# Deferred sums, roots on GpSimd, fewer token riders and one more slot in a fused attention and gated-FFN kernel

## The chip, the cores and the metric

The kernel runs on one core of one Trainium2 chip. The metric is the device time of one execution in microseconds (us); of several runs the median is given. Each engine of the core works through its own queue in order: TensorE (PE) multiplies matrices, VectorE (DVE), ScalarE (ACT) and GpSimd (POOL) work elementwise, and SyncE (SP) issues nearly all transfers.

## The reference

2048 tokens of 512 features are normalised. One branch is a causal attention over a window of 256 keys, with 32 heads of 16 features; the other is a gated FFN with 1792 hidden features. The output is the input plus the product of the attention's projection and the silu of the FFN.

```python
xn = _layernorm(x)
s = _A_ref(xn, A_wqkv, A_wo)                  # softmax over keys i-255..i, then @ wo
g = _silu(_B_ref(xn, B_w1, B_w3, B_w2))       # (silu(xn @ w1) * (xn @ w3)) @ w2
return x + s * g
```

## The kernel before

**Numbers.** Every fp32 operand is held as a sum of two scaled fp16 numbers, high and low, and each dense product is three fp16 products (high-high, high-low, low-high). The split is done by ACT (high part) and by DVE or POOL (low part, a subtraction in two halves of 256 columns, L304).

**Tiles.** There are four token tiles t of 512 tokens, four groups g of 8 heads, and two halves p of a group: 32 *units* (t, g, p). A unit has two attention passes. Pass 1 (L575) computes scores with queries on the partitions and takes their maxima on DVE (L607). Pass 2 (L648) computes the scores again with keys on the partitions, adds masks on DVE (L676), takes exponentials on ACT (L679), and multiplies by the values into a PSUM tile of two banks called po (L697), of which there is one buffer. Pass 1 of a unit runs two units ahead of its pass 2. Pass 1 writes its scores to the tile s, which has two buffers, or, for the kinds marked "X" in the plan (L1065 and on), to po while that is free.

**A unit's end.** `finish` (L703) has ACT copy the first bank of po to os (L707), DVE add the second (L710), and SP store four blocks to the tile on (L716) and the denominators to DRAM (L717). With the second half of a group, `normalise` (L727) loads the denominators back; 8 steps later DVE inverts them (L734, L735) and they are broadcast by eight transfers to rb (L741); 24 steps later POOL has multiplied, and ACT and POOL split the result for the output projection (L747).

**Order.** PE's order is the order in which the program is written; the other engines' instructions are put in order by a scheduler when the program is built, by readiness and priority (`urgent`, L134, raises it). The program interleaves each unit's batches of scores with *dense pieces* of the FFN, projections and outputs (`spread`, L1097). Each batch and each piece is a *step*; `later(n, f)` (L140) emits f after n steps. The FFN's hidden features come in 14 blocks f: `gate_up` (L862), then `down` in four groups of blocks (L911), whose results are evicted at L932 and L935. In the first token tile the weights are loaded, measured (squares on ACT, L232 and L820) and split, and the split ones are stored to DRAM (dW); the later token tiles load them from there, `load` (L761) two blocks ahead: two tiles of w1 and w3 (L765) and one of w2 (L766).

**Slots.** Weights, products and sums share a pool of 39 slots of 2 KB a partition (`take`, L109), which are given back at a step of the program and taken oldest first. A transfer into a slot waits on SP until the slot's last readers have ended.

**Later tokens.** `prepare_beside` (L481) brings in token tiles 1 to 3 beside the units: loads, statistics (L404, L405), `rstd` (L407, a reciprocal square root by an integer guess, L409 to L414, and two steps of refinement on DVE, L416 to L424), centring (L427), and the transposition by small matmuls (L465) which *ride* on the unused columns of a pass-1 score tile, with two DVE instructions each (L474, L475). Which score tile takes a rider is decided in `pass1` (L596 to L603): one that finds `alone[0]` set; it is cleared by a rider unless the group's number t*4+g is at most 4.

Of the kernel before, what the change touches and what calls it, by code (L numbers as in the profile page):

```python
# [10 lines left out]
F32 = mybir.dt.float32  # L11
# [38 lines left out]
TWO_ONES = struct.unpack("f", struct.pack("ee", ONE, ONE))[0]  # L50
VW = DH + 1
VB = 10
SLOTS = 39
ORDERED = {ENGINE.PE}
GROUPS = ((0, 4), (4, 8), (8, 11), (11, 14))

# [23 lines left out]
def tile_block(ctx: ExitStack, tc: tile.TileContext, x, wqkv, wo, w1, w3, w2, out):  # L80
# [53 lines left out]
    def urgent():  # L134


        return tc.high_priority(offset=200) if started else nullcontext()
    made_so_far = [0]

    def later(n, f):  # L140
        made_so_far[0] += 1
        queue.append((now[0] + n, made_so_far[0], f))
# [249 lines left out]
    def prepare(t):  # L392

        mv = lnpool.tile([P, 4, 2], F32, name="mv")
        rs = lnpool.tile([P, 4], F32, name="rs")
        xts = {}

        def load(b):
            xts[b] = take(F32)
            (nc.scalar if t == 0 and b % 2 else nc.sync).dma_start(xts[b], x[t * TW + b * P:t * TW + (b + 1) * P, :])  # L400

        def stats(b):
            st = lnpool.tile([P, nc.vector.BN_STATS_DIM], F32, name="st")
            nc.vector.bn_stats(st, xts[b])  # L404
            nc.vector.bn_aggr(mv[:, b, :], st)  # L405

        def rstd(b0, b1):  # L407
            ve = lnpool.tile([P, b1 - b0], F32, name="ve")
            nc.vector.tensor_scalar(ve, mv[:, b0:b1, 1], 1e-5, None, op0=ALU.add)  # L409


            r0 = lnpool.tile([P, b1 - b0], F32, name="r0")
            nc.vector.tensor_scalar(r0.bitcast(I32), ve.bitcast(I32), 1, None, op0=ALU.logical_shift_right)
            nc.vector.tensor_scalar(r0.bitcast(I32), r0.bitcast(I32), -1.0, float(0x5F3759DF), op0=ALU.mult, op1=ALU.add)  # L414
            sq = lnpool.tile([P, b1 - b0], F32, name="sq")
            nc.vector.tensor_mul(sq, r0, r0)  # L416
            nc.vector.tensor_mul(sq, sq, ve)

            nc.vector.scalar_tensor_tensor(sq, sq, -10 / 3, sq, op0=ALU.add, op1=ALU.mult)
            nc.vector.scalar_tensor_tensor(r0, sq, 5.0, r0, op0=ALU.add, op1=ALU.mult)  # L420
            with nullcontext() if t else tc.issue_after(lasts["cast"].ins):
                nc.vector.tensor_mul(sq, r0, r0)
            nc.vector.scalar_tensor_tensor(sq, sq, -0.5 * (3 / 8)**3 * XS, ve, op0=ALU.mult, op1=ALU.mult)
            nc.vector.scalar_tensor_tensor(rs[:, b0:b1], sq, 1.5 * (3 / 8) * XS, r0, op0=ALU.add, op1=ALU.mult)  # L424

        def centre(b):
            lasts["centre"] = nc.vector.tensor_scalar(xts[b], xts[b], mv[:, b, 0:1], rs[:, b:b + 1],  # L427
                                                      op0=ALU.subtract, op1=ALU.mult)

        def turn(b):  # L430
            if t not in X:
                X[t] = xpool.tile([P, NC, TW], F16, name="XH"), xpool.tile([P, NC, TW], F16, name="XL")
            xh, xl = X[t]
            c = slice(b * P, (b + 1) * P)

            if b < 2:
                pt = bank([P, NC, P])
            elif b == 2:
                pt = pso.tile([P, 2, TW], F32, name="po")[:, 0, :].rearrange("p (k q) -> p k q", q=P)
            else:  # L440
                pt = scores_bank()[:, 0, :].rearrange("p (k q) -> p k q", q=P)
            for k in range(NC):
                nc.tensor.transpose(pt[:, k, :], xts[b][:, k * P:(k + 1) * P], identf)
            give(xts.pop(b))
            with urgent():
                lasts["xh"] = nc.scalar.copy(xh[:, :, c], pt)

            def rest():
                turned[t] = turned.get(t, 0) + 1
                with urgent():  # L450
                    lasts["x"] = nc.vector.tensor_sub(xl[:, :, c], pt, xh[:, :, c])
            later(1, rest)

        def turn_beside(b, n, s):


            if t not in X:
                X[t] = xpool.tile([P, NC, TW], F16, name="XH"), xpool.tile([P, NC, TW], F16, name="XL")
            xh, xl = X[t]
            for k in range(n, n + 2):  # L460
                for h in range(2):
                    for c in range(2):
                        f = k * P + 64 * c
                        rows = slice(64 * h, 64 * h + 64)
                        nc.tensor.matmul(s[64 * c:64 * c + 64, h, WIN + 64 * (k - n):WIN + 64 * (k - n + 1)],  # L465
                                         xts[b][rows, f:f + 64], identf[rows, rows], start=True, stop=True)
            if n:
                give(xts.pop(b))

            def rest():  # L470
                pt = s[:, :, WIN:WIN + P].rearrange("p h (k q) -> p k h q", k=2)
                hi, lo = (a[:, n:n + 2, b * P:(b + 1) * P].rearrange("p k (h q) -> p k h q", h=2) for a in (xh, xl))
                with urgent():
                    nc.vector.tensor_copy(hi, pt)  # L474
                    nc.vector.tensor_sub(lo, pt, hi)  # L475
                if n:
                    turned[t] = turned.get(t, 0) + 1
            return rest
        return load, stats, rstd, centre, turn if t == 0 else turn_beside
# [95 lines left out]
    def pass1(t, g, p):  # L575
# [6 lines left out]
        def part(ii, a, beside, narrow):  # L582
# [17 lines left out]
                maxima.clear()  # L600
            elif alone[0] and besides:
                after = [besides.pop(0)(s)]
            alone[0] = not after or t * NG + g <= NG  # L603
            for r in range(2):
                junk = ppool.tile([P, D], BF16, name="junk", bufs=1)
                with urgent():
# [41 lines left out]
    def pass2(t, g, p):  # L648
# [52 lines left out]
                        begun.add((h, i))  # L701

        def finish():  # L703
            os = opool.tile([P, TW], F32, name="os")
            po = cell["po"]
            with urgent():
                nc.scalar.copy(os, po[:, 0, :])  # L707

                c = slice(0 if t else 64, TW)
                nc.vector.tensor_add(os[:, c], os[:, c], po[:, 1, c])  # L710
            if p == 0:
                ON[t, g] = (opool.tile([P, TW], F32, name="on", bufs=1), dpool.tile([8, TW], F32, name="dd"))
            on, dd = ON[t, g]
            for i in range(4):
                h = (i // 2) * 4 + 2 * p + i % 2
                nc.sync.dma_start(on[16 * h:16 * h + 16, :], os[32 * i:32 * i + 16, :])  # L716
            nc.sync.dma_start(dd[4 * p:4 * p + 4, :], os[DH::32, :])  # L717
            if p == 1:
                normalise(t, g)

        def last(*cs):
            values(*cs)
# [37 lines left out]

    def load(t, f):  # L761
        if t:
            WF[t, f] = a, b = [take(F16) for _ in range(2)], take(F16)
            for k in range(2):
                nc.sync.dma_start(a[k], dW1[f, k])  # L765
            nc.sync.dma_start(b, dW2[f])  # L766
            return
        RAW[f] = raw = [take(F32) for _ in range(2)]
        for k, w in enumerate((w1, w3)):
            nc.sync.dma_start(raw[k].rearrange("p (c f) -> p c f", f=P),  # L770
                              w[:, f * P:(f + 1) * P].rearrange("(c p) f -> p c f", p=P))
# [34 lines left out]
    RAW2 = {}  # L806
    NORMS = {}

    def load_down(f):
        RAW2[f] = raw = take(F32)  # L810
        nc.sync.dma_start(raw, w2[f * P:(f + 1) * P, :])

# [184 lines left out]
    def feed_forward():  # L997
# [3 lines left out]
        for t in range(NT):  # L1001
            for f in range(FB):
                if t == 0:

                    if (f % 2 or f == 0) and f + LEAD < FB - 2:
                        pieces += [(0, lambda f=f: load(0, f)) for f in (range(f + LEAD, f + LEAD + 2) if f else range(4, LEAD + 1))]
                    elif f + LEAD == FB - 1:
                        pieces += [(0, lambda f=f: load(0, f)) for f in range(FB - 2, FB)]
                    if f % 2 and f + 3 < FB:
                        pieces.append((0, lambda f=f + 3: measure(f, 1)))  # L1010
                    pieces += [(0, lambda f=f: load_down(f)) for f in range(f + 2 if f else 0, min(f + 3, FB))]
                    for m in range(f + 1 if f else 0, min(f + 2, FB)):
                        k = next(k for k, (_, f1) in enumerate(GROUPS) if m < f1)
                        pieces.append((0, lambda k=k, m=m: later(2, lambda: measure_down(k, m))))
                else:
                    if f == 0:
                        pieces += [(0, lambda t=t, f=f: load(t, f)) for f in range(2)]
                    if f + 2 < FB:
                        pieces.append((0, lambda t=t, f=f + 2: load(t, f)))
                if f == FB - 4 and t + 2 < NT:  # L1020
                    first, second = prepare_beside(t + 2)
                    pieces += first
# [267 lines left out]
```

## Time and profile before

| | us |
|---|---|
| runs | 836.98, 834.78, 833.58 (median 834.78) |
| profiled execution | 833.8 |
| its span, first to last instruction | 832.0 |
| PE busy in the span | 805.9 |
| DVE busy | 611.5 |
| ACT busy | 406.3 |
| POOL busy | 197.8 |

The profile comes from one execution. A line of the timeline gives start, duration, engine, source line, operation and tiles; a last bracket tells how long the engine stood idle before it, and what ended that. A line of the groups gives the count, the busy time and the mean in ns of one instruction, then the idle time ahead of them. A line of busy times by stretch gives each engine's busy time and count, then the share of full speed that was granted to PE's clock (PEclk), the transfers' share and GB/s. Line numbers are of the kernel before.

### The profile page before, as it was taken

The page shows a single profiled execution, that of the slowest core. Times are in us where ns is not written, and L with a number is a line of the kernel's source. Part 1 is how long each engine was busy: PE and PEld are TensorE (multiplying, and loading weights), DVE is VectorE, ACT ScalarE, POOL GpSimd, SP SyncE. Part 2 cuts the span into 40 slices and gives each one's busy share as a digit, 9 for nine tenths or more (in the row PEclk, how much of TensorE's full clock was granted, in tenths as well). Part 3 has the DMA queues.
Part 4 walks back from the last instruction along what each step waited for, and adds up shares of the span by engine and source line. Part 5 has one row for each costly group of instructions (what it writes and reads, how often), then busy time and mean ns, then how long its engine had stood idle before and what let it go on. Part 6 is the DMA issues. An engine that isn't in the chain of part 4 may idle for free.

```text
span 832.0 us, 22921 instructions
## 1 busy us (share of the span) xinstructions
PE 805.9 (97%) x8924; PEld 380.1 (46%) x8924; DVE 611.5 (74%) x2010; ACT 406.3 (49%) x594; POOL 197.8 (24%) x325
## 2 busy tenths in 40 slices
PE   8989898899999999999999999999999999999998
PEld 4434344444444444444444444444444444444444
DVE  8788768866797667797778876687777887676435
ACT  6889595463536544344433444453444443443521
POOL 2237164141313203111110211121111104031211
PEclk9999999999999999999999999999999999999999
DMA  9977565157533454443442435543453452434101
GB/s 286 270 228 227 183 195 163 43 155 223 171 109 77 110 145 122 138 138 107 132 126 68 131 103 151 146 117 101 119 144 86 114 140 86 120 92 130 52 20 53
DMA packets 95324, 110.65 MB, mean 133 GB/s; under 512 B 17200, under 2 KB 60528, under 8 KB 95216
## 3 DMA queue, kind: packets, MB, share of 16 engines
q1 hardware_dynamic: 94928, 108.67, 45.7%
q8 instruction: 70, 1.15, 0.6%
q10 hardware_dynamic: 288, 0.52, 0.2%
q14 instruction: 38, 0.31, 0.1%
HBM read 76.28 MB, written 28.57 MB: 126 GB/s over the span
## 4 chain that ended last, share of the span: by engine, by line
PE 65%; DVE 11%; DMA 9%; ACT 6%; issue 4%; SPq 3%; POOL 2%; POOLq 0%; ACTq 0%; DVEq 0%
PE m L862 25%; PE m L911 12%; PE po L697 7%; PE m L537 6%; PE m L961 4%; PE s L669 4%; DMA slot<-in_B_w_dram 3%; DVE junk L607 3%; PE m L507 3%; PE s L593 2%; POOL slot L304 2%; DVE s L676 2%; ACT slot L307 1%; ACT pt L679 1%; PE po L593 1%
## 5 line engine op out<-in xcount | busy, mean ns | idle before, releaser
L304 POOL TENSOR_TENSOR slot<-slot,slot 128x256 f16<-128x256 f32 (+1 forms) x228 | 149.3, 683 | 571.9 <-ACT slot L890 464.4
L862 PE MATMUL m<-XH,slot 128*128 128x512 f16 x896 | 267.4, 380 | 5.8 <-DVE slot L932 1.9
L679 ACT ACTIVATE pt<-s,es 128x1024 f32<-128x1024 f32 x152 | 167.6, 1113 | 184.7 <-DVE s L676 175.4
L862 PEld LDWEIGHTS <-slot 128*128 128x128 f16 x1344 | 124.9, 98 | 162.0 <-issue 17.5
L862 PE MATMUL m<-XL,slot 128*128 128x512 f16 x448 | 169.8, 379 | 0.0
L911 PE MATMUL m<-slot,slot 128*128 128x512 f16 x672 | 156.4, 380 | 2.1 <-DVE slot L935 0.6
L676 DVE TENSOR_TENSOR s<-s,MK 128x256 f32<-128x256 f32 (+2 forms) x280 | 118.5, 435 | 45.8 <-PE s L669 41.1
L607 DVE CUSTOM_DVE_ANT_0 junk<-s,MW 128x320 bf16<-128x320 f32 x276 | 134.1, 486 | 24.1 <-PE s L593 16.3
L911 PEld LDWEIGHTS <-slot 128*128 128x128 f16 x672 | 62.1, 98 | 80.8 <-issue 9.8
L607 DVE CUSTOM_DVE_ANT_0 junk<-po,MW 128x320 bf16<-128x320 f32 x172 | 83.6, 486 | 5.2
L697 PE MATMUL po<-pt,V 64*32 64x320 f32 (+4 forms) x2880 | 77.2, 342 | 0.0
L890 ACT CAST slot<-slot 128x512 f16<-128x512 f32 x56 | 34.5, 617 | 70.4 <-DVE slot L886 70.0
L697 PEld LDWEIGHTS po<-pt,V 64*32 64x32 f32 x2880 | 50.6, 106 | 22.1 <-issue 0.8
L669 PE MATMUL s<-qa,KA 50*64 50x320 f16 (+3 forms) x1472 | 58.0, 259 | 2.7 <-DVE M L607 1.0
L881 DVE SCALAR_TENSOR_TENSOR slot<-slot,m 128x512 f32<-128x512 f32 x56 | 38.3, 684 | 29.7 <-ACT slot L877 28.7
L669 PEld LDWEIGHTS <-KA 50*64 50x64 f16 x1472 | 30.2, 105 | 57.0 <-issue 35.6
L877 ACT ACTIVATE slot<-m,sgs 128x512 f32<-128x512 f32 x56 | 38.3, 684 | 26.1 <-PE m L862 25.8
L593 PE MATMUL s<-KA,qa 48*64 48x320 f16 (+3 forms) x824 | 45.3, 294 | 4.8 <-ACT pt L679 2.3
L710 DVE TENSOR_TENSOR os<-os,po 128x512 f32<-128x512 f32 (+1 forms) x32 | 21.5, 671 | 36.6 <-ACT os L707 34.9
L935 DVE SCALAR_TENSOR_TENSOR slot<-m,dsc,slot 128x512 f32<-128x512 f32 x48 | 35.9, 747 | 15.6 <-PE m L911 15.3
L886 DVE SCALAR_TENSOR_TENSOR slot<-m,slot 128x512 f32<-128x512 f32 x56 | 38.5, 688 | 11.2 <-PE m L862 10.4
L537 PE MATMUL m<-XH,whi 128*128 128x512 f16 x120 | 45.2, 385 | 1.2 <-DVE slot L886 0.6
(152 smaller groups left out, 886.3 us busy)
## 6 DMA issues: line engine op xcount, KB each, us to landing
slot<-dW SPq DMA_DIRECT2D x126, 256.0 KB
slot<-in_B_w_dram SPq DMA_DIRECT2D x42, 256.0 KB
dW<-slot SPq DMA_DIRECT2D x42, 256.0 KB
slot<-in_A_x_dram SPq DMA_DIRECT2D x30, 256.0 KB
KA<-dK SPq DMA_DIRECT2D x24, 288.0 KB
qa<-dQ SPq DMA_DIRECT2D x32, 192.0 KB
dQ<-slot SPq DMA_DIRECT2D x16, 256.0 KB
dK<-slot SPq DMA_DIRECT2D x16, 256.0 KB
```

What stands on the lines that cost most here:

```text
L304: op(out[:, c], a[:, c], b[:, c])
L537: nc.tensor.matmul(cell["pp"], a[:, k, c, :], b[:, c, :], start=(c, i) == parts[0][0], stop=(c, i) == parts[-1][-1])
L593: nc.tensor.matmul(s[c:c + w, r, :n], qa[rows, 2 * p + a, ii * P + c:ii * P + c + w], ka[rows, 2 * p + a, e - n:e], start=True, stop=True)
L607: nc.vector.tensor_tensor_reduce(out=junk[:, :n], in0=s[:, r, :n], in1=mask, scale=1.0, scalar=NEG, op0=ALU.add, op1=ALU.max, accum_out=M[ ...
L669: nc.tensor.matmul(s[64 * h:64 * h + 64, r, o:o + 64 * n], ka[rows, 2 * p + a, 64 * (m + 4):64 * (m + 5)], qa[rows, 2 * p + a, 64 * (m + k ...
L676: nc.vector.tensor_add(v, v, MK[:, kind, of:of + n, :].unsqueeze(1).to_broadcast([P, 2 * len(which), n, 64]))
L679: nc.scalar.activation(pt, s, AF.Exp, scale=es)
L697: nc.tensor.matmul(cell["po"][32 * i:32 * i + 32, h, 64 * (m + k):64 * (m + k + n)], V[64 * h:64 * h + 64, (4 * t + m // 2) % VB, hd * VW: ...
L862: nc.tensor.matmul(cell[k], w[:, (a * NC + c) * P:(a * NC + c + 1) * P], b[:, c, :], start=c == 0 and i == 0, stop=c == NC - 1 and i == 2)
L877: nc.scalar.activation(sg, cell[0], AF.Tanh, scale=sg_scale[:, f:f + 1])
L886: nc.vector.scalar_tensor_tensor(sg, cell[1], 0.5 * HS / (WS * XS)**2, sg, op0=ALU.mult, op1=ALU.mult)
L911: nc.tensor.matmul(ps, hh[:, a * TW + b * P:a * TW + (b + 1) * P], w[:, c * D:(c + 1) * D], start=f == f0 and i == 0, stop=f == f1 - 1 and ...
```

## The change

Four things are changed. A unit's add, stores and normalising are emitted two steps after ACT's copy instead of at once, and os has one buffer. For token tiles 1 to 3 the refinement of the reciprocal square root is ten instructions on POOL instead of seven on DVE; DVE keeps the integer guess and the centring. Riders share a batch up to group number 2 instead of 4. There are 40 slots, and the later token tiles load a block's w2 tile at the block's own turn instead of two blocks ahead.

```diff
-SLOTS = 39
+SLOTS = 40
...
             sq = lnpool.tile([P, b1 - b0], F32, name="sq")
...
+            if t == 0:
...
+                return
+
+            pool = nc.gpsimd
+            u = lnpool.tile([P, b1 - b0], F32, name="u")
+            pool.tensor_mul(sq, r0, r0)
+            pool.tensor_mul(sq, sq, ve)
+            pool.tensor_scalar(u, sq, -10 / 3, None, op0=ALU.add)
+            pool.tensor_mul(sq, sq, u)
+            pool.tensor_scalar(sq, sq, 5.0, None, op0=ALU.add)
+            pool.tensor_mul(r0, r0, sq)
+            pool.tensor_mul(sq, r0, r0)
+            pool.tensor_mul(sq, sq, ve)
+            pool.tensor_scalar(sq, sq, -0.5 * (3 / 8)**3 * XS, 1.5 * (3 / 8) * XS, op0=ALU.mult, op1=ALU.add)
+            pool.tensor_mul(rs[:, b0:b1], sq, r0)
...
-            alone[0] = not after or t * NG + g <= NG
+            alone[0] = not after or t * NG + g <= 2
...
         def finish():
-            os = opool.tile([P, TW], F32, name="os")
+            os = opool.tile([P, TW], F32, name="os", bufs=1)
             po = cell["po"]
             with urgent():
                 nc.scalar.copy(os, po[:, 0, :])
 
+            def rest():
+
                 c = slice(0 if t else 64, TW)
-                nc.vector.tensor_add(os[:, c], os[:, c], po[:, 1, c])
...
+                with urgent():
+                    nc.vector.tensor_add(os[:, c], os[:, c], po[:, 1, c])
...
+                if p == 1:
+                    normalise(t, g)
+
+            later(2, rest)
...
     def load(t, f):
         if t:
-            WF[t, f] = a, b = [take(F16) for _ in range(2)], take(F16)
+            a = [take(F16) for _ in range(2)]
+            WF[t, f] = [a, None]
             for k in range(2):
                 nc.sync.dma_start(a[k], dW1[f, k])
-            nc.sync.dma_start(b, dW2[f])
             return
...
-    def load_down(f):
+    def load_down(t, f):
+        if t:
+            WF[t, f][1] = b = take(F16)
+            nc.sync.dma_start(b, dW2[f])
+            return
...
+
+                    pieces.append((0, lambda t=t, f=f: load_down(t, f)))
```

More of the change, by code (lines that the diff above doesn't have):

```diff
@@ L415, in rstd @@
             sq = lnpool.tile([P, b1 - b0], F32, name="sq")
[L416 to L424, printed above, removed]
+            if t == 0:
+                nc.vector.tensor_mul(sq, r0, r0)
+                nc.vector.tensor_mul(sq, sq, ve)
+                nc.vector.scalar_tensor_tensor(sq, sq, -10 / 3, sq, op0=ALU.add, op1=ALU.mult)
+                nc.vector.scalar_tensor_tensor(r0, sq, 5.0, r0, op0=ALU.add, op1=ALU.mult)
+                with tc.issue_after(lasts["cast"].ins):
+                    nc.vector.tensor_mul(sq, r0, r0)
+                nc.vector.scalar_tensor_tensor(sq, sq, -0.5 * (3 / 8)**3 * XS, ve, op0=ALU.mult, op1=ALU.mult)
+                nc.vector.scalar_tensor_tensor(rs[:, b0:b1], sq, 1.5 * (3 / 8) * XS, r0, op0=ALU.add, op1=ALU.mult)
+                return
[11 more added lines that the diff above has]
+            pool.tensor_mul(rs[:, b0:b1], sq, r0)
         def centre(b):
@@ L707, in finish @@
                 nc.scalar.copy(os, po[:, 0, :])
+            def rest():
                 c = slice(0 if t else 64, TW)
-                nc.vector.tensor_add(os[:, c], os[:, c], po[:, 1, c])
[L711 to L719, printed above, removed]
+                with urgent():
+                    nc.vector.tensor_add(os[:, c], os[:, c], po[:, 1, c])
+                if p == 0:
+                    ON[t, g] = (opool.tile([P, TW], F32, name="on", bufs=1), dpool.tile([8, TW], F32, name="dd"))
+                on, dd = ON[t, g]
+                for i in range(4):
+                    h = (i // 2) * 4 + 2 * p + i % 2
+                    nc.sync.dma_start(on[16 * h:16 * h + 16, :], os[32 * i:32 * i + 16, :])
+                nc.sync.dma_start(dd[4 * p:4 * p + 4, :], os[DH::32, :])
+                if p == 1:
+                    normalise(t, g)
+            later(2, rest)
         def last(*cs):
@@ L1010, in feed_forward @@
                         pieces.append((0, lambda f=f + 3: measure(f, 1)))
-                    pieces += [(0, lambda f=f: load_down(f)) for f in range(f + 2 if f else 0, min(f + 3, FB))]
+                    pieces += [(0, lambda f=f: load_down(0, f)) for f in range(f + 2 if f else 0, min(f + 3, FB))]
                     for m in range(f + 1 if f else 0, min(f + 2, FB)):
```

## The prediction

> **What bounds the kernel now.** I read the page first, then the busy times by stretch, the waits, and then the timeline of each engine at the places where TensorE (PE) stands still.
>
> ```profile
> span 832.0 us, 22921 instructions
> PE 805.9 (97%) x8924; PEld 380.1 (46%) x8924; DVE 611.5 (74%) x2010; ACT 406.3 (49%) x594; POOL 197.8 (24%) x325
> ```
> ```profile
> core 0: us, PE busy (x) PEld busy (x) DVE busy (x) ACT busy (x) POOL busy (x), PEclk, DMA share, GB/s
> 80.00:100.00 20.00, 15.97 (x181) 7.37 (x179) 15.68 (x51) 14.00 (x30) 6.72 (x10) 1.00 0.61 199
> 140.00:160.00 20.00, 16.28 (x178) 7.86 (x171) 17.47 (x67) 8.15 (x14) 2.42 (x4) 1.00 0.26 85
> 220.00:240.00 20.00, 18.93 (x284) 10.04 (x283) 16.74 (x55) 6.54 (x8) 4.00 (x6) 1.00 0.46 129
> 360.00:380.00 20.00, 18.01 (x214) 8.17 (x215) 17.02 (x55) 7.88 (x10) 5.37 (x8) 0.91 0.31 85
> 480.00:500.00 20.00, 20.00 (x284) 9.91 (x283) 15.80 (x49) 9.41 (x12) 2.60 (x4) 1.00 0.37 99
> ```
>
> PE is the bound: it is idle for 832.0 - 805.9 = 26.1 us of the whole span. The stretch at 480 is the steady state, with no idle PE at all. So whatever the change does to VectorE (DVE) and the queues is worth something only where PE waits: in the first pass over the hidden blocks (4.0 us idle from 80 to 100, 3.7 from 140 to 160), a little at 220 (1.1), and once later, at 360 (2.0, with the granted clock down to 0.91). Added matmul work there is none: the built program has the same number of PE instructions, some dense pieces in another place.
>
> **The deferred sums: nothing on DVE.** DVE's order is set when the program is built, by readiness, not by the place in the source. Reading the built orders side by side, the three rows ahead of the add (L710, now L728) and the three behind it are the same in 29 of 32 units; in the other three (7, 11 and 18, counted from 0) a neighbour or two have changed. It still stands ahead of the next unit's first mask. The four stores and the denominators' store follow the add on the SP queue as before; os having one buffer makes ScalarE's (ACT) next copy wait for these stores, which go out within some 6 us, against 22 us from one unit to the next. I take 0 us. What does move is what is counted from the sum: inversion and split of the normalised tile, two steps later. For the last unit the built orders of the tail are row for row the same, so nothing is late there.
>
> **The roots on GpSimd (POOL).** Seven DVE instructions go for each of the three later token tiles, ten come on POOL, each waiting for the one ahead; the first centring on DVE waits for the tenth. No row shows a 128x4 operation on POOL:
>
> ```profile
> L304 POOL TENSOR_TENSOR slot<-slot,slot 128x256 f16<-128x256 f32 x204 | 132.4, 678 | 524.6 <-ACT slot L890 464.4 <-ACT slot L308 56.6 <-DMA slot<-in_B_w_dram 3.7
> masks.py:199 POOL TENSOR_SCALAR_AFFINE_SELECT identf<-identf 128x128 f32<-128x128 f32 x1 | 0.3, 292 | 0.0
> L1279 POOL MEMSET const-float32-0.0<- 128x1 f32 x1 | 0.1, 98 | 0.2 <-issue 0.2
> ```
>
> So the chain, W, lies between 10 x 0.098 = 1.0 us and 10 x 0.678 = 6.8 us. The 4-wide operation is nearest to the 1-wide one; I take 0.2 each, as for the 0.16 + 0.04 of a dependent DVE one below: W = 2.0 us. Both ends are kept for the range. What it does at the three places:
>
> *Tile 1, at 78 us.*
>
> ```profile
> 78.41 0.17 DVE L414 TENSOR_SCALAR r<-r 128x4 int32<-128x4 int32 x1
> 80.24 0.65 DVE L419 SCALAR_TENSOR_TENSOR sq<-sq 128x4 f32<-128x4 f32 x1
> 82.82 0.59 DVE L422 TENSOR_TENSOR sq<-r 128x4 f32<-128x4 f32 x1
> 84.08 0.60 DVE L424 SCALAR_TENSOR_TENSOR rs<-sq,r 128x4 f32<-128x4 f32 x1
> 80.19 6.72 POOL L304 TENSOR_TENSOR slot<-slot,slot 128x256 f16<-128x256 f32 x10 [3.00 <-ACT slot L308]
> 147.75 0.16 DVE L416 TENSOR_TENSOR sq<-r 128x4 f32<-128x4 f32 x1
> ```
> ```profile
> 88.95 0.25 PE L593 MATMUL s<-KA,qa 48*64 48x128 f16 x4 [1.50 <-DVE M L607]
> 93.79 0.38 PE L862 MATMUL m<-XH,slot 128*128 128x512 f16 x1 [1.89 <-DVE slot L932]
> ```
> ```profile
> 90.47 0.63 ACT L820 ACTIVATE sqa<-slot 128x512 bf16<-128x512 f32 x1 [1.59 <-DMA slot<-in_B_w_dram]
> 91.86 0.57 ACT L707 COPY os<-po 128x512 f32<-128x512 f32 x1
> ```
> ```profile
> 86.94 0.33 SPq L811 DMA_DIRECT2D slot<-in_B_w_dram  x1
> ```
>
> Five of the seven (three are shown) cost some 0.6 us here instead of 0.16: POOL subtracts without a break from 80.19 to 86.9, and they stand beside it. DVE loses 5 x 0.6 + 2 x 0.2 = 3.4 us of work. Against that, POOL is idle until 80.19, so the chain runs from 78.6 to 80.6, while DVE, having done the masks and maxima ahead of the first centring, gets there at 80.24 - 0.3 = 79.9: a wait of 0.7. The maxima that hold PE up at 88.95 come some 2.7 us earlier, and the 1.50 goes.
>
> By the Trainium skill, page "SBUF — State Buffer", section "Who interferes with whom", a DVE instruction with two SBUF inputs or in a two-port mode and a GpSimd one that reads SBUF lock each other out for a whole instruction. These rows fit (0.59 beside 0.16); were the stretch not this lock, the five would be worth 1.0 us instead of 3.0.
>
> What is late next is 93.79: PE waits for an eviction that stands behind the add of unit 0, which waits for ACT's copy at 91.86, which stands behind a square that waited 1.59 us for a weight load, issued at 86.94. That one is the price here. The load was issued when the last pair of POOL's run freed its buffer (80.19 + 6.72 = 86.91). With 40 slots the buffer it gets is freed by the pair before, 1.3 us earlier, and the roots ahead push that pair by 0.4 or less (80.6 against 80.19). I take 1.3 - 0.4: **-0.9 us**, which takes in the 1.50, as PE waits at 93.79 in any case. Bounds: -1.3, and at W = 6.8 a wait of 5.5 for a saving of 3.4, +2.1.
>
> *Tile 2, at 147 us.* Seven at 0.2 go (1.4 us); an eviction of 0.7 now stands between L414 and the centring, so the wait is W - 0.7 = 1.3, and the maxima and the tokens' second halves come up to 1 us late before they catch up. DVE is the bound here (17.47 of 20 us). **-0.1 us**; bounds -1.1 (W = 1.0: wait 0.3) and +4.7.
>
> *Tile 3, at 366 us.*
>
> ```profile
> 367.20 0.64 DVE L416 TENSOR_TENSOR sq<-r 128x4 f32<-128x4 f32 x1
> 368.86 0.53 DVE L424 SCALAR_TENSOR_TENSOR rs<-sq,r 128x4 f32<-128x4 f32 x1
> 369.42 2.23 DVE L427 TENSOR_SCALAR slot<-slot,mv,rs 128x512 f32<-128x512 f32 x4
> ```
> ```profile
> 367.59 0.33 PE L593 MATMUL s<-KA,qa 48*32 48x320 f16 x8 [0.24 <-ACT pt L679]
> 372.65 0.41 PE L669 MATMUL s<-qa,KA 50*64 50x256 f16 x8 [0.99 <-DVE M L607]
> 373.82 0.33 PE L593 MATMUL s<-KA,qa 48*64 48x320 f16 x4 [0.76 <-DVE M L607]
> ```
> ```profile
> 372.00:374.00 2.00, 0.59 (x12) 0.26 (x12) 1.73 (x9) 0.00 (x0) 0.00 (x0) 1.00 0.00 0
> 374.00:376.00 2.00, 2.00 (x11) 0.80 (x8) 1.99 (x5) 0.00 (x0) 0.47 (x1) 0.78 0.01 4
> 376.00:378.00 2.00, 2.00 (x6) 0.73 (x5) 0.95 (x5) 1.11 (x1) 0.94 (x2) 0.50 0.26 55
> 378.00:380.00 2.00, 2.00 (x15) 0.76 (x17) 0.69 (x1) 0.60 (x1) 0.00 (x0) 0.87 0.45 152
> ```
>
> Before, roots and four centrings (367.20 to 371.65) delayed the maxima and PE lost 0.99 + 0.76 = 1.75 us; the gap was followed by a granted clock of 0.78, 0.50 and 0.87, which cost another 2 x (0.22 + 0.50 + 0.13) = 1.7. In the new order the first centring stands *ahead* of four masks. DVE waits the whole W there, then does one centring (0.55); the exponentials behind the masks come some 2.2 us later, and at 367.59 PE was already waiting 0.24 for one. So the stall moves rather than goes: 2.2 for 1.75. I let the clock fall as before: **+0.4 us**. Without that fall it is -1.3, and with W = 1.0 as well, -2.3; at W = 6.8 it is +5.2.
>
> The Trainium skill, "TensorE: Matmul & The Clock Gate", Part 1, has the clock halved by a monitor with a free-running window of 3.4 us. These rows agree with about 3.4 us at 0.50. As the window's phase is free, by that rule a stall of 2.2 us may or may not be followed by it: the two values above.
>
> **Tokens ride on one scores tile a batch.** Their matmuls into the unit's output bank (po), which has one buffer, go from 11 groups to 7; all four are of tile 2, near 217 to 242 us.
>
> ```profile
> 228.26 0.33 PE L593 MATMUL po<-KA,qa 48*64 48x320 f16 x4 [1.07 <-DVE XL L475]
> ```
>
> That one goes: **-1.1 us**, the idle PE of the stretch at 220. The riders spread over units 6 and 7, on the double-buffered bank, where the rows show no such wait. Bounds 0 and -1.2.
>
> **40 slots and the later w2 loads.** In the steady state no PE wait is on a load, so loading w2 two blocks later is 0 there. In the first pass one w2 load now stands 17 places earlier on SP, ahead of the broadcasts, and its square on ACT moves ahead too:
>
> ```profile
> 140.17 0.62 ACT L820 ACTIVATE sqa<-slot 128x512 bf16<-128x512 f32 x1
> 141.55 0.56 ACT L707 COPY os<-po 128x512 f32<-128x512 f32 x1
> 143.49 1.46 PE L911 MATMUL m<-slot,slot 128*128 128x512 f16 x6 [0.62 <-DVE slot L935]
> ```
>
> One of two squares ahead of unit 2's copy goes (0.76 us from one start to the next), so the add and the eviction behind it come that much earlier, and PE's 0.62 goes: **-0.6 us** (bounds 0 and -0.8).
>
> **Sum.** -0.9 - 0.1 + 0.4 - 1.1 - 0.6 = -2.3 us. The profiled execution took 833.8 us, 1.8 of them around its span of 832.0; so 831.5. The median of the runs is 834.8, 1.0 more, which I add: **832.5 us**.
>
> **Rivals.**
> 1. *A larger gain.* The clock doesn't fall near 374, W is 1.0, and the earlier loads and the lighter DVE also remove stalls that I left alone (PE is idle 7.7 us in the two stretches at 80 and 140). For it: DVE is busy 17 of 20 us there. Against: ACT and the loads hold those stalls too. The lower bounds sum to -1.3 - 1.1 - 2.3 - 1.2 - 0.8 = -6.7; with 1.6 of those stalls it is 826.5 on the median.
> 2. *Nothing.* The sums don't move, and what the roots give at tile 1 is waited for elsewhere (the load at 86.94 is not earlier): only the po rider and the square stay, against tile 3: about 834.
> 3. *Slower: the POOL chain holds DVE.* DVE's balance over the three places is 3W - 2.0 (the waits: W - 1.3, W - 0.7, W) less 3.4 + 1.4 + 2.2 = 7.0 saved. It turns at W = 3.0, that is 0.30 for each of the ten. At 0.678 each it is +11.4, and PE follows, as masks and maxima stand behind the centring; with the -1.7 of rider and square, 844.
>
> **How the numbers follow.** The forecast case, 830 to 834: 0.45. The larger gain 0.22, nothing 0.18, slower 0.15. The range is **826.5 to 838**: below, rival 1; above, W at about 4.5, short of the far end, since the widest row is 64 times as wide as these operations. About 0.5% (4.2 us, so below 830.6 or above 839.0) is what can be told from no change. Faster takes rival 1 and a part of the forecast: 0.35; slower 0.15; the rest 0.50.
>
> **What would show it.** DVE's first L442 of tiles 1 to 3 should start where POOL's L439 ends; start-to-start of L430 to L439 gives W at once. PE's wait at 93.79 for L956 should be some 1 us shorter, with the w2 load ahead of it earlier; the 0.62 at 143 and the 1.07 at 228 gone; near 367 a wait of about 2 us on exponentials, none at 372. The add should be where it was in DVE's order. W beyond 3 us, a clock that falls at another place, or a dense order that meets a bank still held would make it wrong.

## The result and the profile after

The changed kernel takes **847.04 us** (median of 6 runs, 845.07 to 849.43) against 834.6 us (833.58 to 836.98, 6 runs) before. The ratio is 1.0144, with a 95% interval of 1.0123 to 1.0165: 12.4 us slower. The forecast was 832.5 us, in a range up to 838.

The head of the page after, and the busy times of the same five stretches that the prediction shows of before (their columns: PE, its weight loads, DVE, ACT and POOL busy, granted clock, transfers):

```profile
span 843.2 us, 22914 instructions
PE 811.3 (96%) x8924; PEld 383.2 (45%) x8924; DVE 606.5 (72%) x1989; ACT 406.0 (48%) x594; POOL 205.8 (24%) x355
```
```profile
80.00:100.00 20.00, 16.73 (x179) 7.41 (x177) 13.40 (x42) 13.61 (x29) 7.82 (x14) 0.91 0.59 193
140.00:160.00 20.00, 15.44 (x161) 7.38 (x154) 14.81 (x53) 6.42 (x10) 3.35 (x12) 0.83 0.18 58
220.00:240.00 20.00, 19.10 (x258) 9.65 (x253) 15.13 (x52) 6.81 (x9) 5.23 (x8) 1.00 0.41 114
360.00:380.00 20.00, 16.69 (x162) 7.67 (x162) 15.26 (x48) 7.72 (x11) 4.71 (x14) 0.98 0.50 148
480.00:500.00 20.00, 19.65 (x281) 9.94 (x279) 15.94 (x49) 9.88 (x13) 3.06 (x4) 1.00 0.44 108
```

DVE is busy for 5 us less than before, and PE stands still for 31.9 us instead of 26.1. PE's busy time has grown by 5.4 us too, without one more matmul: that is the lower clock, at three places now. A lighter engine, and a slower kernel. To find the places, I take wider stretches, first of before, then of after:

```profile
76.00:100.00 24.00, 19.69 (x211) 8.98 (x210) 19.53 (x72) 17.97 (x38) 7.91 (x12) 1.00 0.62 196
140.00:162.00 22.00, 18.28 (x190) 8.69 (x186) 19.36 (x80) 9.15 (x15) 2.60 (x4) 1.00 0.23 77
340.00:364.00 24.00, 24.00 (x273) 11.24 (x271) 19.41 (x63) 7.81 (x9) 1.42 (x2) 1.00 0.58 166
364.00:386.00 22.00, 20.01 (x220) 9.04 (x219) 18.22 (x58) 9.08 (x12) 5.37 (x8) 0.92 0.33 97
440.00:760.00 320.00, 319.59 (x3889) 151.14 (x3874) 240.79 (x759) 137.86 (x169) 59.99 (x90) 1.00 0.42 117
```
```profile
76.00:100.00 24.00, 20.46 (x210) 9.25 (x210) 16.91 (x63) 17.57 (x37) 9.88 (x22) 0.93 0.66 202
140.00:162.00 22.00, 17.43 (x189) 8.36 (x182) 15.91 (x56) 6.79 (x11) 3.35 (x12) 0.84 0.16 52
340.00:364.00 24.00, 21.55 (x239) 9.78 (x238) 16.79 (x53) 7.36 (x8) 2.72 (x4) 0.93 0.48 126
364.00:386.00 22.00, 18.69 (x230) 8.90 (x229) 17.34 (x56) 8.24 (x11) 7.43 (x18) 1.00 0.34 101
440.00:760.00 320.00, 317.10 (x3813) 150.70 (x3812) 239.66 (x754) 137.30 (x169) 60.12 (x89) 1.00 0.43 116
```

What PE loses in a stretch is its idle time plus the length times what is missing from a full clock. (The stretches of the two kernels shift against each other by the time lost ahead of them; each of the first four holds the same event.)

| stretch, us | lost before | lost after | difference |
|---|---|---|---|
| 76–100, roots of tile 1 | 4.3 | 3.5 + 1.7 of clock | +0.9 |
| 140–162, roots of tile 2 | 3.7 | 4.6 + 3.5 of clock | +4.4 |
| 340–364, statistics of tile 3 | 0 | 2.5 + 1.7 of clock | +4.1 |
| 364–386, roots of tile 3 | 2.0 + 1.8 of clock | 3.3 | −0.4 |
| 440–760, steady state | 0.4 | 2.9 | +2.5 |

The sum, 11.5 us, is about the difference of the two profiled executions (845.07 − 833.8 = 11.3; the medians differ by 12.4). Two causes are to be seen in it.

**DVE waits for POOL.** First POOL's timeline at tile 3, its first two rows and the last, then DVE's first centring of each of the three tiles:

```profile
370.64 0.20 POOL L430 TENSOR_TENSOR sq<-r 128x4 f32<-128x4 f32 x1 [22.31 <-DVE r L414]
370.92 0.20 POOL L431 TENSOR_TENSOR sq<-sq,ve 128x4 f32<-128x4 f32 x1
...
373.23 0.20 POOL L439 TENSOR_TENSOR rs<-sq,r 128x4 f32<-128x4 f32 x1
```
```profile
81.12 0.87 DVE L442 TENSOR_SCALAR slot<-slot,mv,rs 128x512 f32<-128x512 f32 x1 [1.57 <-POOL rs L439]
...
148.86 1.00 DVE L442 TENSOR_SCALAR slot<-slot,mv,rs 128x512 f32<-128x512 f32 x2 [2.26 <-POOL rs L439]
...
373.47 0.55 DVE L442 TENSOR_SCALAR slot<-slot,mv,rs 128x512 f32<-128x512 f32 x1 [2.91 <-POOL rs L439]
```

A 128x4 operation takes 0.20 us on POOL, but 0.28 from start to start in a chain: from 370.64 to 373.43 W is 2.8, and 2.9 to DVE's start. And PE behind it, first at tile 1 (the row of before, then that of after), then at tile 2 and at tile 3:

```profile
82.01 1.46 PE L911 MATMUL m<-slot,slot 128*128 128x512 f16 x6 [0.49 <-DVE slot L932]
```
```profile
83.11 1.70 PE L935 MATMUL m<-slot,slot 128*128 128x512 f16 x6 [1.97 <-DVE slot L956]
```
```profile
151.06 0.42 PE L684 MATMUL s<-qa,KA 50*64 50x320 f16 x10 [2.44 <-DVE mt L643]
151.88 0.30 PE L608 MATMUL s<-KA,qa 48*64 48x256 f16 x4 [0.40 <-ACT pt L694]
...
153.57 0.48 PE L608 MATMUL po<-KA,qa 48*64 48x320 f16 x4 [1.16 <-DVE XL L490]
```
```profile
378.36 0.33 PE L608 MATMUL s<-KA,qa 48*32 48x320 f16 x8 [2.24 <-ACT pt L694]
379.37 0.33 PE L608 MATMUL s<-KA,qa 48*32 48x320 f16 x8 [0.67 <-ACT pt L694]
```

**DVE waits for a transfer, with a sum behind it.** DVE's timeline near 354, and PE's row there:

```profile
354.39 1.29 DVE L404 BATCH_NORM_STATS2 st<-slot 128x6 f32<-128x512 f32 x2 [4.09 <-DMA slot<-in_A_x_dram]
355.59 0.67 DVE L728 TENSOR_TENSOR os<-os,po 128x512 f32<-128x512 f32 x1
...
356.33 0.72 DVE L959 SCALAR_TENSOR_TENSOR slot<-m,dsc,slot 128x512 f32<-128x512 f32 x1
```
```profile
357.11 1.33 PE L935 MATMUL m<-slot,slot 128*128 128x512 f16 x3 [2.45 <-DVE slot L959]
```

Two statistics of tile 3 stand *ahead* of the sum of unit 11 on DVE and wait 4.09 us for the tokens' load. Sum and eviction (L959) wait with them, and PE waits for the eviction. Before, the sum came first (at 346.64, the statistics at 357.15). No wait of PE is on a w2 tile.

### The profile page after: what moved, and what is told of

Same layout as the page of the kernel before. It is cut to its first block, busy times and chain, and to the rows that moved or that the text cites. A ratio compares the mean times of both kernels' runs of the same rounds, so it can differ in the third digit from the quotient of the medians.

```text
span 843.2 us, 22914 instructions
## 1 busy us (share of the span) xinstructions
PE 811.3 (96%) x8924; PEld 383.2 (45%) x8924; DVE 606.5 (72%) x1989; ACT 406.0 (48%) x594; POOL 205.8 (24%) x355
## 5 line engine op out<-in xcount | busy, mean ns | idle before, releaser
L304 POOL TENSOR_TENSOR slot<-slot,slot 128x256 f16<-128x256 f32 (+1 forms) x228 | 151.3, 691 | 532.4 <-ACT slot L914 413.8
L935 PE MATMUL m<-slot,slot 128*128 128x512 f16 x672 | 158.2, 382 | 6.0 <-DVE slot L959 2.4
L959 DVE SCALAR_TENSOR_TENSOR slot<-m,dsc,slot 128x512 f32<-128x512 f32 x48 | 35.8, 747 | 13.1 <-PE m L935 12.9
```

The lines of the kernel that those rows point to most:

```text
L304: op(out[:, c], a[:, c], b[:, c])
L935: nc.tensor.matmul(ps, hh[:, a * TW + b * P:a * TW + (b + 1) * P], w[:, c * D:(c + 1) * D], start=f == f0 and i == 0, stop=f == f1 - 1 and ...
```

## The experiments

Theory A: the loss has two causes that add. DVE stands still for the POOL chain at tiles 1 to 3; and loading w2 at the block's own turn changes the order that is built for DVE and ACT, so that they wait where they did not. The deferred sums, the riders and the slot do nothing that can be measured. The rivals (B: the chain is all; C: the clock falls strike wherever PE has a gap, so that no edit brings its share; D: the deferred sums; E: the 40th slot; the others where they come) are in the expectations. Each run is compared with the kernel before on the same chip: 833.5 us for runs 1 to 4 and 9 to 12, 834.5 for runs 5 to 8. Between the two groups a difference of a microsecond means nothing.

**1. Roots back on DVE.** In the changed kernel:

```diff
+            nc.vector.tensor_mul(sq, r0, r0)
...
-            pool.tensor_mul(sq, r0, r0)
...
-            pool.tensor_mul(rs[:, b0:b1], sq, r0)
...
+            nc.vector.scalar_tensor_tensor(rs[:, b0:b1], sq, 1.5 * (3 / 8) * XS, r0, op0=ALU.add, op1=ALU.mult)
```

> The changed kernel with the roots of tiles 1 to 3 back on DVE; sums, riders, slots and w2 loads stay as changed. Theory A (three places, two causes: the waits of DVE for the POOL chain near 80 and 150 us, and the statistics that stand ahead of the sum of unit 11 near 354 us): the roots cost 0.9 + 4.4 - 0.4 = 4.9 us, so 847.0 - 4.9 = 842, and the wait of PE for L959 near 354 stays at 2.5 us. Rival B (the chain is the whole loss, as in the forecast's slower rival): 835. Rival C (clock falls strike wherever PE has a gap; an edit takes one away and another comes): 845 to 847.

Measured: 839.76 us, 1.0062 of before (1.0042 to 1.0082). What the kernel takes over before falls from 12.4 to 6.3 us: the roots hold half of the loss, somewhat more than A said, and not all of it. Rivals B and C are out. PE's longest wait near 150 is 1.16 us now, where it was 2.44.

**2. w2 two blocks ahead again.** In the changed kernel:

```diff
+            nc.sync.dma_start(b, dW2[f])
...
-                    pieces.append((0, lambda t=t, f=f: load_down(t, f)))
```

> The changed kernel with the w2 tile of later tokens loaded two blocks ahead again, still 40 slots; roots on POOL. In the built order the two statistics of tile 3 stand behind the sum of unit 11 again. Theory A: the gap of 2.45 us near 354 and the clock behind it (1.7) go, 847.0 - 4.1 = 843; if the 2.5 us that are idle after 440 us come from the w2 loads too, 840.5. Rival B (the chain is the whole loss): 847, no change. Rival D (the deferred sums are at fault near 354): the gap stays, 847.

Measured: 838.72 us, 1.006 (1.0042 to 1.0078). Over before it takes 5.2 us instead of 12.4: more goes than the 4.1 of the one place, and rather more than with the idle time after 440 us. DVE's rows there, of this kernel:

```profile
348.19 0.69 DVE L728 TENSOR_TENSOR os<-os,po 128x512 f32<-128x512 f32 x1 [0.44 <-ACT os L722]
...
358.43 1.28 DVE L404 BATCH_NORM_STATS2 st<-slot 128x6 f32<-128x512 f32 x2
```

The sum is first, and the statistics wait for nothing.

**3. Both.** Left of the change: the deferred sums, the riders and the slot.

> Roots on DVE and w2 two ahead, so of the change only the deferred sums with one os buffer, the riders and the 40th slot are left. Theory A: 847.0 - 4.9 - 4.1 = 838, or 835.5 if the idle time after 440 us belongs to the w2 loads. If the parts left gain what the prediction gave them (1.7 us): 833. Rival D (the deferred sums cost): 838 or more, with DVE's sums later than ACT's copy.

Measured: 832.74 us, 0.999 (0.9975 to 1.0004). The two causes hold all but 1.3 us of the loss: 832.74 + 6.0 (run 2 less this) + 7.0 (run 1 less this) = 845.7, against 847.0. The pair differing only in the roots (run 2, then this one) shows where the roots cost time; its profiled executions, 837.26 and 833.65 us, differ by only 3.6 of the 6.0 us:

```profile
76.00:100.00 24.00, 19.60 (x212) 9.05 (x212) 17.47 (x66) 17.91 (x37) 10.20 (x22) 1.00 0.62 194
140.00:162.00 22.00, 17.77 (x163) 8.45 (x162) 16.55 (x60) 6.76 (x11) 3.99 (x14) 0.84 0.14 44
```
```profile
76.00:100.00 24.00, 21.24 (x219) 9.70 (x218) 20.87 (x80) 19.21 (x41) 8.13 (x13) 1.00 0.62 202
140.00:162.00 22.00, 18.80 (x193) 8.86 (x199) 20.06 (x80) 7.75 (x11) 1.56 (x3) 0.92 0.11 34
```

With idle time and clock these two stretches hold 1.6 and 2.8 us (2.76 idle in this run against 4.40 in run 2; 3.20 + 1.76 of clock against 4.23 + 3.52), and that from 364 to 386 another 0.9; the rest of the execution gives 1.7 back. DVE is busy for 3.4 and 3.5 us *less* with the roots on POOL, and PE loses time all the same.

**4. Sums at once.** In the changed kernel:

```diff
-            later(2, rest)
+            rest()
```

> The changed kernel with a unit's add, stores and normalising emitted at once behind ACT's copy, one os buffer kept. In the built order the statistics of tile 3 stand ahead of the sum of unit 11 as they do in the changed kernel. Theory A: the deferral moves nothing, 847 within 1.5 us, with the gap near 354 in place. Rival D: the deferral is what costs near 354 and after 440 us, 840.

Measured: 845.83 us, 1.0156 (1.0135 to 1.0176), which is the changed kernel within the spread of runs. The wait near 354 stays, at 351.99:

```profile
351.99 1.29 DVE L404 BATCH_NORM_STATS2 st<-slot 128x6 f32<-128x512 f32 x2 [3.56 <-DMA slot<-in_A_x_dram]
353.19 0.67 DVE L728 TENSOR_TENSOR os<-os,po 128x512 f32<-128x512 f32 x1
```

So it isn't the deferral that let the statistics pass the sum. Rival D falls.

**5. The kernel before with the roots on POOL alone.** The edit is that of the change.

> The kernel before with one edit: the roots of tiles 1 to 3 as ten instructions on POOL. Theory A (the cost is DVE's wait for the chain, wherever it stands): the difference of the two earlier runs that differ only in the roots, 838.7 - 832.7 = 6.0 us, so 833.5 + 6.0 = 839.5. Rival E (the roots cost only in the order that the 40th slot makes at tile 2): 834 to 836.

Measured: 841.54 us, 1.007 (1.0045 to 1.0094). The roots cost 7 us by themselves, without the 40th slot. Rival E is out for them.

**6. The kernel before with w2 at its own turn alone.**

> The kernel before with one edit: the w2 tile of later tokens loaded at the block's own turn, 39 slots. In the built order one statistic of tile 3 (in the changed kernel two) stands ahead of the sum of unit 11. Theory A (DVE waits there for a transfer, and its order after 440 us changes too): 839.8 - 832.7 = 7.0 us were lost with two ahead; with one, whose load lands sooner, 4 to 7, so 837.5 to 840.5. Rival E (the loss needs the 40th slot): 834.

Measured: 838.65 us, 1.0047 (1.0034 to 1.006), so +4.2, at the lower end of A's span. Rival E is out here too: the loss needs no 40th slot, though with it the loss was 7.0. The places are not the ones expected. The single statistic ahead of the sum waits 2.29 us, at 348.75, but PE loses only 0.4 us from 340 to 364; 4.2 us are lost between 440 and 760, where the kernel before loses 0.4:

```profile
440.00:760.00 320.00, 315.83 (x3761) 149.25 (x3764) 236.38 (x744) 137.09 (x168) 60.93 (x90) 1.00 0.41 116
```

One such place is to be seen on ACT, first in the changed kernel, with PE's row behind it, then at the same place in run 2 (w2 two ahead):

```profile
739.43 0.63 ACT L979 ACTIVATE slot<-slot 128x512 f32<-128x512 f32 x1 [1.48 <-POOL slot L304]
739.97 2.10 ACT L694 ACTIVATE pt<-s,es 128x1024 f32<-128x1024 f32 x2
```
```profile
742.12 0.33 PE L608 MATMUL s<-KA,qa 48*32 48x320 f16 x8 [0.67 <-ACT pt L694]
```
```profile
731.31 2.12 ACT L694 ACTIVATE pt<-s,es 128x1024 f32<-128x1024 f32 x2 [0.47 <-DVE s L691]
735.05 0.63 ACT L979 ACTIVATE slot<-slot 128x512 f32<-128x512 f32 x1 [1.62 <-POOL slot L304]
```

The tanh of the output (L979) waits for its slot, whose last reader is a subtraction on POOL. It waits 1.5 to 1.6 us in both kernels; but in one the two exponentials stand behind it, and PE waits 0.67 for the second of them (at 742.12), and in the other they stand ahead of it. That is one place of several. With 40 slots and w2 at its own turn (the changed kernel and runs 1, 4 and 9) PE has two waits of 0.67 and 0.73 us and one of 0.42 at the same lines and places each time; before and in runs 2 and 3 none is above 0.23. So this loss goes with the turn of the w2 loads, but that all of it comes from changes of order is not shown place by place.

**7. Roots on POOL, centrings later.** Run 2 with the centring kept behind the maxima last emitted:

```diff
-            lasts["centre"] = nc.vector.tensor_scalar(xts[b], xts[b], mv[:, b, 0:1], rs[:, b:b + 1],
...
+            with tc.issue_after(lasts["max"].ins) if t else nullcontext():
+                lasts["centre"] = nc.vector.tensor_scalar(xts[b], xts[b], mv[:, b, 0:1], rs[:, b:b + 1],
```

> Roots on POOL, w2 two ahead (838.7 so far), and each centring of tiles 1 to 3 put on DVE behind the maxima emitted last ahead of it, so that DVE has other work while POOL makes its ten steps. Theory A (the wait of DVE at the first centring is the cost): the gaps of PE near 148 and 373 us go, at most 833, and near 829 if the cluster of four centrings was costing in the kernel before too. Rival F (POOL's ten operations cost by themselves, or the cost is carried elsewhere): 837 to 839.

Measured: 832.86 us, 0.9981 (0.9967 to 0.9995). The chain on POOL is the same, and its cost is nearly gone: the kernel is 1.6 us below the one before, where run 2 was 5.2 above. Not all of this is the wait for POOL, since the later centrings gain some 1.9 us with the roots on DVE too (run 8 against run 3, each by its distance from before). But with the later centrings, roots on POOL and roots on DVE are only 1.0 us apart, and their intervals overlap. So it is not POOL's ten operations by themselves that cost, it is DVE's place behind them. Rival F falls.

In the stretches of tiles 2 and 3 PE lost 1.2 and 0.7 us, against 7.8 and 4.9 in run 2. The 829 did not come, since tile 1 now had a gap of 3.83 us at 93.64 and one of 2.22 at 118.10, and the clock fell behind each.

**8. The same with the roots on DVE.**

> The same later centrings with the roots on DVE and w2 two ahead (832.7 without them). Theory A: the wait for POOL is not there to be taken away; what goes is the cluster of centrings near 147 and 371 us, with PE's gaps of 1.15 + 1.32 and 1.38 + 0.93 us and the two clock falls behind them (about 1.7 each): 829, and within 1 us of the run with the roots on POOL. Rival G (the clock falls come at another gap): 832.

Measured: 831.88 us, 0.9971 (0.9959 to 0.9984), 1.0 from run 7, as A said, but 3 above its 829: the clusters (four centrings in a row on DVE) at tiles 2 and 3 went, but at tile 1 the gap of 0.90 us that before has at 115.71 became one of 2.23 at 116.56, with a fall of the clock.

**9. Statistics behind the sum.** Run 1 (roots on DVE, w2 at its own turn) with

```diff
-            nc.vector.bn_stats(st, xts[b])
+            with tc.issue_after(lasts["add"].ins) if t == 3 else nullcontext():
+                nc.vector.bn_stats(st, xts[b])
```

> Roots on DVE and w2 at its own turn, as in the run at 839.8, with one edit: the statistics of tile 3 are issued behind the sum emitted last ahead of them, which puts them behind the sum of unit 12, so DVE waits for no transfer ahead of a sum. Theory A (the order on DVE near 354 us is what the later w2 loads cost there): PE's gaps of 1.9 and 1.5 us and the clock behind them go, 839.8 - 4.5 = 835.3; the 2 us that are idle after 440 us stay. Rival H (PE is late there because of the loads themselves): 839.8.

Measured: 833.52 us, 0.9995 (0.9981 to 1.0009), 6.2 less than run 1. w2 is loaded at the block's own turn as there; the edit is on DVE's order. Rival H falls. Run 1, then this one:

```profile
340.00:364.00 24.00, 20.38 (x223) 9.14 (x222) 17.00 (x54) 6.70 (x8) 1.42 (x2) 0.95 0.43 126
```
```profile
340.00:364.00 24.00, 24.00 (x275) 11.23 (x272) 18.36 (x57) 8.08 (x10) 1.42 (x2) 1.00 0.52 143
```

3.6 us of idle time and 1.2 of clock go in the first stretch; the 2.7 us that run 1 loses between 440 and 760 stay (2.6), as expected of an edit that touches only tile 3. From 364 to 386, 0.8 us are lost against 1.3 in run 1. (The two profiled executions differ by 4.8 us, the medians by 6.2.)

**10 and 11. Deferred sums alone, and riders alone, in the kernel before.**

> The kernel before with the deferred sums and one os buffer alone. The prediction and Theory A: 0 us, 834.5 within 1.5. Rival D (deferring costs a step of the normalising or a buffer): 838.

> The kernel before with riders sharing a batch up to group 2 only. The prediction: the wait of 1.07 us near 228 goes, 834.5 - 1.1 = 833.4. Rival I (another rider meets a busy bank, or the idle time only moves): 834.5.

Measured: 833.99 us, 0.9995 (0.9979 to 1.001), and 832.85 us, 0.9988 (0.9973 to 1.0002). Neither can be told from no change. Of the riders' 1.07 us the stretch from 224 to 234 gives back 0.7: PE is busy there for 9.61 of 10 us, where it was 8.93. In the changed kernel it is 9.10: there two other waits, of 0.51 and 0.39 us, stand at 228.21 and 230.44.

**12. Later centrings at tiles 2 and 3 only.** Run 8 with `if t > 1` for `if t`.

> Roots on DVE, w2 two ahead, later centrings for tiles 2 and 3 only (with tile 1 too: 831.9). Theory A: at tile 1 the later centrings brought a gap of 2.4 us near 114 where 1.1 stood before, and a clock of 0.96 from 100 to 140 (1.6 us); these go, the 1.7 near 88 comes back: 830 to 831. Rival G (clock falls come wherever a gap is): 832.

Measured: **829.4 us**, 0.9947 (0.9927 to 0.9966). It beats the kernel before by 4.1 us and the changed one by 17.6. It has the deferred sums, the riders and the slot of the change, not its roots and not its w2 loads, and the four centrings of a tile no longer stand together:

```profile
140.00:162.00 22.00, 19.77 (x264) 10.02 (x263) 19.70 (x82) 10.02 (x16) 2.60 (x4) 1.00 0.16 50
...
364.00:386.00 22.00, 21.55 (x266) 10.24 (x265) 18.65 (x59) 9.96 (x13) 4.65 (x8) 1.00 0.35 94
```

2.2 and 0.4 us are lost there, against 3.7 and 3.8 before.

## Why the prediction was wrong

| term | forecast | found |
|---|---|---|
| deferred sums | 0 | 0 (runs 4 and 10) |
| tile 1 | −0.9 | idle −0.8, clock +1.7 |
| tile 2, with the square | −0.7 | idle +0.9, clock +3.5 |
| tile 3 | +0.4 | −0.4 |
| riders | −1.1 | −0.6 (run 11, within its interval) |
| later w2 loads | 0 | +7.0 (run 1 less run 3), +4.2 alone |

**The step that failed first: "loading w2 two blocks later is 0 there".** I asked only whether PE waits for a load, and no row shows that it does, before or after. But the loads are part of what the build puts in order. With the w2 loads at their own turn, SP issued tile 3's first tokens ahead of the stores of unit 11's sum instead of behind them, and so earlier (the row of before, then that of after),

```profile
351.65 0.43 SPq L400 DMA_DIRECT2D slot<-in_A_x_dram  x1
```
```profile
348.76 3.17 SPq L400 DMA_DIRECT2D slot<-in_A_x_dram  x2
```

and the built order put two statistics ahead of that sum, as if their data were there. They were not, by 4.09 us. (How the scheduler came to this order no run shows; that the order cost the time, run 9 does.) The prediction had it in hand: unit 11 was one of the three whose neighbours it saw change, and "a neighbour or two have changed" was priced at nothing, without asking what the new neighbour waits for. It was also booked under the wrong part: runs 4 and 10 show that the deferral has no hand in it.

**The step that failed second: the break-even of the POOL chain, "it turns at W = 3.0".** The waits themselves came as worked out: with W = 2.9 the forms W − 1.3, W − 0.7 and W give 1.6, 2.2 and 2.9, and the rows show 1.57, 2.26 and 2.91. W was taken as 2.0, from DVE's 0.16 + 0.04 for a dependent operation; on POOL it is 0.20 and a gap of 0.08. That was a size within the stated bounds. But at W = 2.9 the balance of DVE, 6.7 of waiting against 7.0 of work saved, still came out even, and the kernel lost 6 to 7 us (run 2 less run 3, and run 5). The balance is the mistake: work saved in seven small pieces among other instructions gave PE little, while a wait in one block stops the masks, maxima and token copies behind it, and PE with them. At tile 1 an eviction that PE was already waiting for at 82.01 stood behind the waiting centring, and the 0.49 us became 1.97; the prediction had priced the waits at 88.95 and 93.79 and not this one. At tile 2 PE stood for 2.44 + 0.40 + 1.16 us. Rival 3, at 0.15, had the mechanism of this half of the loss, but set its point of decision too high. That its 844 came near 847 is luck: it was worked out for W = 6.8, and the other half of the loss is the w2 loads, which it did not have.

**The clock** was let fall once, as before. In the profiled execution it fell at three places, for some 6.9 us in all against 1.8: nearly half of what the kernel lost there. (The six executions have mean clocks of 0.990 to 0.995, so this share differs from one to the next.)

**Right:** at 93.79 PE's wait is shorter by 0.75 (1.14 at 93.92, forecast 1 us), the 1.50 of the maxima, the 0.62 at 143 and the 1.07 at 228 are gone (the last with two others in its place), the stall of tile 3 moved from the maxima to the exponentials, and the sum's deferral cost nothing.

## What to carry to other kernels

Where a scheduler sets an engine's order, an edit that only moves a transfer can reorder instructions on engines that never touch it: for each reordered pair ask what the one that is now in front waits for, and who stands behind it. Work moved to an idle engine was free here only where its consumer had other work in front of it; a wait in one block cost more than the same time of small operations spread out, and moving the consumer (run 7) cured what moving the work had broken.

## What the runs showed of the hardware

The clock falls in whole windows of 3.41 us, whose borders run on through the execution. In the profiled execution of the changed kernel it fell at 84.18, 152.45 and 357.25 us: 68.27 and 273.07 after the first, which is 20 and 80 times 3.413. Busy times by such windows:

```profile
80.77:84.18 3.41, 1.44 (x7) 0.57 (x6) 3.06 (x8) 3.41 (x7) 3.33 (x7) 1.00 0.16 36
84.18:87.59 3.41, 3.41 (x62) 1.65 (x68) 3.38 (x11) 3.15 (x9) 3.41 (x6) 0.50 1.00 375
149.04:152.45 3.41, 0.95 (x30) 0.66 (x30) 3.41 (x16) 1.11 (x1) 0.00 (x0) 1.00 0.01 2
152.45:155.86 3.41, 2.29 (x24) 1.28 (x25) 3.41 (x14) 1.63 (x3) 0.00 (x0) 0.50 0.26 84
...
374.32:377.73 3.41, 1.46 (x6) 0.57 (x6) 2.42 (x8) 1.67 (x3) 2.38 (x4) 1.00 0.63 211
377.73:381.14 3.41, 2.10 (x80) 1.50 (x87) 3.38 (x9) 2.67 (x4) 0.94 (x3) 1.00 0.02 5
```

A window in which PE was idle for 1.97 us is followed by one at half clock, which costs 1.7 us; the idle time from 374 to 381, 3.3 us, is cut in two by a border, with 1.95 and 1.31 on its sides, and is followed by none. The fall at 152.45 went on for a second window, after 1.12 us idle in the first. Over the thirteen profiled executions in which it fell, every window at full clock with 1.97 us or more of idle PE was followed by a half-clock window, none with 1.62 or less was, and in between it went both ways. So a gap is dear from about half a window on, and its place against the border decides: two gaps that each cost about 1 us can cost 1.7 more if they share a window, as the 0.99 and 0.76 us of before did near 373. The Trainium skill, "TensorE: Matmul & The Clock Gate", Part 1, has the free-running window of 3413 ns, with which these rows agree; it has the clock fall after at least one idle window, and here about half of one was enough. If that means a window without any work, a stall of 2.2 us would never bring a fall; these rows, not that rule, bear out the prediction's two values for it.
